# Attention scores and weight transposes of a fused attention and expert kernel, cut in halves of 64 queries

## The chip, the cores and the metric

The kernel runs on one core of one Trainium2 chip. The metric is the device time of one execution in microseconds. TensorE (PE in the profile) does the matmuls; its weight loads are listed as PEld. VectorE is DVE, ScalarE is ACT, GpSimd is POOL, and SP is the queue that issues most of the DMAs. PSUM is the memory that matmuls write.

## What is computed

Three stages follow one another: attention over pooled keys and values, a dense layer with an ELU, and a layer of eight experts of which each token uses one.

```python
B, H, S, D = 8, 8, 576, 64
k_p = k.reshape(B, H, 72, 8, D).mean(axis=3)      # v_p likewise
scores = (1 / 8) * q @ k_p.T                       # 576 x 72 per batch and head
attn = softmax(scores)
x = (attn @ v_p) laid out as 4608 x 512            # tokens x (heads * 64)
h = x @ w_in;  y = elu(h) @ w_out                  # 512 -> 2048 -> 512
e = argmax(y @ w_gate)                             # one of 8 experts
out = gate * relu(y @ w1[e]) @ w2[e]
```

Everything is float32 in and out. The two dense layers multiply in three products of a high and a low part; scores, transposes and the product with the values are plain float32 matmuls.

## The kernel before

**Tiles.** The 4608 tokens are 36 query tiles of 128 tokens. A batch has 576 = 4.5 x 128 tokens, so tiles 4, 13, 22 and 31 hold 64 queries of one batch and 64 of the next; the other 32 belong to one batch. Three query tiles make a block of 384 tokens, and a block has 16 steps, one for each 128 columns of the hidden layer.

**Attention of a tile t.** `s_mm` (L405) multiplies the queries `qT` (stationary, heads in pairs: one head of a pair on partitions 0 to 63, the other on 64 to 127) with the pooled keys `kT` (72 columns move) into two PSUM banks `sp`, one for each half of the partitions. `parts(t)` gives one run of 128 queries, or two runs of 64 for the four tiles that straddle two batches. DVE takes the maxima (L414), ACT the exponentials (L423), DVE normalises (L427 to L429). `t_mm(t, hh)` (L435) transposes the 128 x 72 weights of four heads into one bank `aTp`; it is called for `hh` 0 and 1. `t_copy` (L441) copies each bank to SBUF as `aT`. `pv_mm` (L450) multiplies `aT` with the pooled values into a bank `pv`, and `pv_copy` (L463, L464) splits that into the block's `xh` and `xl`.

**Order.** The order on every engine of this phase is the order in which the code is written. `first_block` does tiles 0 to 2, and the scores of tile 3. Then `step(n)` issues: the 12 matmuls of the first dense layer into `h` (`g1_mm`, L477), the slot `pe_mid`, the activations on ACT (L487 to L489) and DVE (L494, L495), the slot `act_mid`, the 9 matmuls of the second dense layer into `y` for step n - 2 (`g2`, L519), the slot `pe_end`, and so on. A table fills the slots: from tile 9 on, scores stand in `pe_mid` of step s, transposes in `pe_mid` of step s + 3, their two copies in `act_mid` of that step, behind the activations, and `pv_mm` in its `pe_end`. So TensorE has in such a step: `h`, transposes, `y`, `pv`. Tiles 6 to 8 have places of their own (transposes in `pe_end`). During the first 28 steps DVE and ACT also decode the dense weights (`dec`, `raw`, L217 to L242).

**Banks.** `bank` hands out three PSUM banks in turn (and, in the first block, three more) to scores, transposes and `pv`. A tile takes two for scores, two for transposes and one for `pv`.

The last third of the time is the expert stage (lines from 1000 on), which the change does not touch.

Of the kernel before, what the change touches and what calls it, by code (L numbers as in the profile page):

```python
# [19 lines left out]
P = 128  # L20
B, H, S, D = 8, 8, 576, 64
POOLW = 8
SP = S // POOLW
# [27 lines left out]
NT_MAIN = 3  # L51
NU_MAIN = 3
UT = P // 4
SIDES = (5, 6, 8)

C_ID = 0
# [17 lines left out]
def constants():  # L74
# [13 lines left out]
    c[:, C_E:C_E + NE] = e  # L88
    c[:, C_J] = p // UT
    c[p, C_SUM + SUM_AT + p // POOLW] = 1  # L90
# [4 lines left out]
def fused_kernel(ctx: ExitStack, tc: tile.TileContext, q, k, v, w_in, w_out, w_gate, w1, w2, cst, out):  # L95
    nc = tc.nc
# [10 lines left out]
    ident = cpool.tile([P, P], F32, name="ident")  # L107
# [63 lines left out]
    kTs = [apool.tile([P, 4, SP], F32, name=f"kT{i}") for i in range(2)]  # L171
# [104 lines left out]
    def bank(shape, name):  # L276
        early["n"] += 1
        if early["bank"] and early["n"] % 2:
            return bank_y(shape, name)
        return bank_a(shape, name)  # L280
# [90 lines left out]
    banks = {}  # L371

    qTs, ss, aTs = {}, {}, {}
    xh, xl = {}, {}

    def parts(t):
        r0 = t * P
        b0 = r0 // S
        n0 = min(P, (b0 + 1) * S - r0)
        res = [(b0, r0 - b0 * S, 0, n0)]  # L380
        if n0 < P:
            res.append((b0 + 1, 0, n0, P - n0))
        return res
# [9 lines left out]
    def s_mm(t):  # L393
        ss[t] = (
            work([P, H, SP], "s", f"s{t}"),
            ring(apool, [P, H], F32, "mx", 3, f"mx{t}"),
            ring(apool, [P, H], F32, "sm", 3, f"sm{t}"),
        )
        ps = [bank([P, 4, SP], f"sp{t}_{o}") for o in range(2)]
        qT = qTs.pop(t)  # L400
        for pr in range(4):
            for b, s0, p0, n in parts(t):
                for o in range(2):
                    os = slice(D * o, D * (o + 1))
                    nc.tensor.matmul(  # L405
                        ps[o][p0:p0 + n, pr], qT[os, pr, p0:p0 + n], kTs[b % 2][os, pr], start=True, stop=True
                    )
        for o in range(2):
            banks["s", t, o] = ps[o]
        if t < 6:  # L410
            w_free(f"qT{t}")
# [16 lines left out]
        nc.vector.reciprocal(sm, sm)  # L428
        nc.vector.tensor_mul(s, s, sm.unsqueeze(2).to_broadcast([P, H, SP]))  # L429

    def t_mm(t, hh):
        s = ss[t][0]
        ps = banks["t", t, hh] = bank([P, 4, P], f"aTp{t}_{hh}")
        for h in range(4):
            nc.tensor.transpose(ps[:SP, h], s[:, 4 * hh + h], ident)  # L435

    def t_copy(t, hh, copy):
        ps = banks.pop(("t", t, hh))
        if hh == 0:
            aTs[t] = work([SP, H, P], "aT", f"aT{t}")  # L440
        copy(aTs[t][:, 4 * hh:4 * hh + 4], ps[:SP])  # L441

    def pv_mm(t):
        aT = aTs.pop(t)
# [220 lines left out]
    def at(n, slot, fn, *args):  # L665
        events.setdefault((n, slot), []).append((fn, args))
# [11 lines left out]
        at(n, "dve_mid" if t in SCORE0 else "end", s_norm, t)  # L678

    def trans_at(t, n):  # L680
        for hh in range(2):
            at(n, "pe_end" if t in OUT else "pe_mid", t_mm, t, hh)
            at(n, "act_end" if t in OUT else "act_mid", t_copy, t, hh, nc.scalar.copy)
        out = OUT.get(t, ((n, "pe_end"), (n + 1, "pre")))
        at(*out[0], pv_mm, t)
        at(*out[1], pv_copy, t)
# [4 lines left out]
    OUT = {  # L691
        6: ((28, "pe_end"), (29, "pre")),
        7: ((29, "pe_end"), (30, "pre")),
        8: ((31, "pe_mid"), (31, "act_mid")),
    }
# [23 lines left out]
    for n, t in enumerate(range(TB, 2 * TB)):  # L719
        if n:  # L720
            at(n, "pe_mid", s_mm, t)
            for hh in range(2):
                at(n, "dve_late", s_max, t, hh)
        for hh in range(2):
            at(n, "act_mid" if n else "pre", s_exp, t, hh)
        at(n, "act_end" if n else "dve_pre", s_norm, t)
        for hh in range(2):
            at(n + 1, "pe_mid", t_mm, t, hh)
            at(n + 1, "act_hi", t_copy, t, hh, (nc.scalar.copy, nc.vector.tensor_copy)[hh])
        at(n + 1, "pe_end", pv_mm, t)  # L730
        at(n + 1, "copies", pv_copy, t)
# [15 lines left out]
    for x, (w, c) in enumerate(chunks):  # L747
        n = 2 + x
# [76 lines left out]
    def first_block():  # L825
# [23 lines left out]
            for hh in range(2):  # L849
                s_max(t, hh)  # L850

        def trans(t):
            for hh in range(2):
                t_mm(t, hh)

        for pr in range(4):
            prep_k(0, pr)
        k_scale(0)
# [16 lines left out]
        exps(2)  # L875
        a_load(5)
        s_norm(0)
        trans(0)
        v_sum(0, range(2, 4))
        w_hi(0, 0)  # L880
        t_copy(0, 0, nc.scalar.copy)
        t_copy(0, 1, nc.scalar.copy)
        w_mul(0, 1, nc.vector.tensor_scalar_mul)
        s_norm(1)
        trans(1)
        v_sum(0, range(4, 5))
        v_sum_copy(0)
        s_norm(2)
        pv_mm(0)
        trans(2)  # L890
        t_copy(1, 0, nc.scalar.copy)
        t_copy(1, 1, nc.scalar.copy)
        w_bits(0, 1)
# [98 lines left out]
    def lists_rest():  # L992
# [5 lines left out]
        nb = new([P, NE], "nb")  # L998
        nc.vector.tensor_scalar(nb, rest, float(UT), None, op0=ALU.is_gt)
        nt = new([P, NE], "nt")  # L1000
# [53 lines left out]
    def m_index(it):  # L1054
# [5 lines left out]
        if kind == "U":  # L1060
            for j in range(4):
                nc.sync.dma_start(oi[UT * j:UT * (j + 1), 0:1], tab[bass.ds(b0, UT), :])
        else:
# [182 lines left out]
    def u_g1(it):  # L1246
# [3 lines left out]
        for c in range(KC):  # L1250
            for j in range(4):
                js = slice(UT * j, UT * (j + 1))
                mark["g1"] = nc.tensor.matmul(
                    ps[js], z[:, c, :UT], raws2[it, j][0][:, c], start=c == 0, stop=c == KC - 1
                ).ins
# [109 lines left out]
    for k in range(1, len(main)):  # L1365
        kind, prev = main[k][0], main[k - 1][0]
        for u in range(TILES[kind]):
            if kind == "T":
                n = 4 * k - 2
            elif prev == "T":  # L1370
                n = 4 * k - TILES[kind] + u
            else:
                n = 4 * k - 1
# [170 lines left out]
```

## Time and profile before

| | us |
|---|---|
| median of 3 runs | 1417.66 |
| lowest, highest run | 1416.53, 1419.87 |
| the profiled execution | 1418.04 |
| its span, first to last instruction | 1416.2 |
| mean granted TensorE clock | 0.995 |

The profiled execution took 1.8 us more than its span, and 0.4 us more than the median. In a timeline row the columns are start, duration, engine, line, operation, names, shapes and count; rows that follow each other with the same names are merged. A matmul's duration includes its modelled way through the array, so matmuls overlap, and what a group costs is read from the start of one group to the start of the next. In brackets stands idle time before the instruction and what ended it.

### The profile page before, as it was taken

The numbers are of one execution on the slowest core, as the hardware profiler recorded it, in microseconds if no ns is written. First come the engines' busy times: TensorE is split into PE (matmuls) and PEld (weight loads), VectorE is DVE, ScalarE is ACT, GpSimd is POOL, SyncE is SP. The second block draws the span as 40 slices with busy tenths as digits, with TensorE's granted clock in tenths as the row PEclk, the third lists the DMA queues.
The fourth block names the chain that finished last, engine by engine and source line by source line (L and its number), as shares of the span: only waits on it lengthen the run. The fifth ranks groups of instructions, "written<-read, shape, count | busy, mean of one in ns | idle before, by whom it ended". The sixth has DMA issues, their size and how long they took to land. (4 is left out here: it accounts for less than half of the span.)

```text
span 1416.2 us, 22675 instructions
## 1 busy us (share of the span) xinstructions
PE 1396.7 (99%) x8113; PEld 1197.3 (85%) x8114; DVE 913.4 (64%) x2152; ACT 741.7 (52%) x1781; POOL 199.1 (14%) x207
## 2 busy tenths in 40 slices
PE   9999999999999999999999999999999999999996
PEld 6798888888888888888888888988888888778785
DVE  6899877876766667576757576886556444434261
ACT  5777755655656556566565565562333333334251
POOL 0011010111111211121210000020222122112020
PEclk9999999999999999999999999999999999999999
DMA  9156435566452552543451332364566456759460
GB/s 344 57 174 198 134 72 97 66 75 99 59 89 47 92 59 49 76 75 67 85 73 53 53 46 46 88 163 105 172 94 205 127 162 240 239 185 330 144 222 23
DMA packets 109141, 169.37 MB, mean 120 GB/s; under 512 B 15510, under 2 KB 53016, under 8 KB 109017
## 3 DMA queue, kind: packets, MB, share of 16 engines
q1 hardware_dynamic: 91528, 135.45, 38.2%
q0 software_dynamic: 17488, 32.37, 11.1%
q8 instruction: 66, 1.08, 0.4%
q14 instruction: 59, 0.48, 0.2%
HBM read 146.35 MB, written 21.88 MB: 119 GB/s over the span
## 5 line engine op out<-in xcount | busy, mean ns | idle before, releaser
L519 PE MATMUL y<-woh,gh 128*128 128x512 f32 x576 | 232.5, 404 | 1.9 <-DVE yr L533 1.9
L519 PE MATMUL y<-woh,gl 128*128 128x512 f32 x576 | 227.5, 395 | 0.0
L519 PE MATMUL y<-wol,gh 128*128 128x512 f32 x576 | 226.1, 392 | 0.0
L494 DVE SCALAR_TENSOR_TENSOR g<-g,th 128x384 f32<-128x384 f32 x192 | 106.6, 555 | 160.7 <-ACT th L489 159.7
L570 DVE SCALAR_TENSOR_TENSOR junk<-yr,wgb 128x512 bf16<-128x512 f32 x264 | 181.2, 686 | 3.5 <-ACT yr L535 1.3
L487 ACT ACTIVATE th<-h 128x384 f32<-128x384 f32 x192 | 94.5, 492 | 165.7 <-PE h L477 165.4
L477 PE MATMUL h<-xh,wih 128*128 128x384 f32 x768 | 170.0, 343 | 1.4 <-ACT xh L463 1.4
L477 PE MATMUL h<-xl,wih 128*128 128x384 f32 x768 | 165.4, 337 | 0.0
L477 PE MATMUL h<-xh,wil 128*128 128x384 f32 x768 | 164.8, 336 | 0.0
L501 ACT CAST gh<-g 128x384 fp32r<-128x384 f32 x192 | 98.9, 515 | 115.7 <-DVE g L495 96.2
L477 PEld LDWEIGHTS h<-xh,wih 128*128 128x128 f32 x768 | 136.8, 189 | 19.5 <-issue 2.7
L1187 DVE SCALAR_TENSOR_TENSOR hlD<-mhD,hhD 128x512 fp32r<-128x512 f32 x64 | 44.2, 690 | 161.4 <-ACT hhD L1186 153.9
L1186 ACT ACTIVATE hhD<-mhD 128x512 fp32r<-128x512 f32 x64 | 38.5, 601 | 199.3 <-PE myD L1209 191.6
L477 PEld LDWEIGHTS h<-xl,wih 128*128 128x128 f32 x768 | 136.6, 188 | 0.2
L477 PEld LDWEIGHTS h<-xh,wil 128*128 128x128 f32 x768 | 136.6, 188 | 0.0
L502 DVE TENSOR_TENSOR gl<-g,gh 128x384 fp32r<-128x384 f32 x192 | 107.1, 558 | 39.9 <-ACT gh L501 36.1
L519 PEld LDWEIGHTS y<-woh,gl 128*128 128x128 f32 x576 | 108.4, 188 | 23.8
L519 PEld LDWEIGHTS y<-woh,gh 128*128 128x128 f32 x576 | 108.3, 188 | 21.1 <-issue 2.4
L519 PEld LDWEIGHTS y<-wol,gh 128*128 128x128 f32 x576 | 108.7, 189 | 16.9
L495 DVE TENSOR_TENSOR g<-g,h 128x384 f32<-128x384 f32 x192 | 106.3, 554 | 6.6
L489 ACT ACTIVATE th<-th 128x384 f32<-128x384 f32 x192 | 100.8, 525 | 6.1
L488 ACT ACTIVATE g<-th 128x384 f32<-128x384 f32 x192 | 100.8, 525 | 6.1
(275 smaller groups left out, 2313.6 us busy)
## 6 DMA issues: line engine op xcount, KB each, us to landing
wgb<-in_moe_w_gate_dram SPq DMA_DIRECT2D x96, 256.0 KB, 4.8
w1stD<-in_moe_w_dram SPq DMA_DIRECT2D x32, 512.0 KB, 3.6
w2stD<-in_moe_w_dram SPq DMA_DIRECT2D x32, 512.0 KB, 7.8
qT<-in_q_dram SPq DMA_DIRECT2D x36, 256.0 KB, 9.6
ybuf<-yr SPq DMA_DIRECT2D x33, 256.5 KB, 7.1
raw<-in_moe_w_in_dram SPq DMA_DIRECT2D x16, 512.0 KB, 7.8
raw<-in_moe_w_out_dram SPq DMA_DIRECT2D x15, 512.0 KB, 8.6
t1U<-in_moe_w_dram SPq DMA_DIRECT2D x12, 512.0 KB, 7.7
```

The lines of the kernel that those rows point to most:

```text
L477: mark["g1"] = nc.tensor.matmul(ps, wi[i][a][:, c, o:o + P], bb[blk][:, c, :], start=n == 0, stop=n == 3 * KC - 1).ins
L487: nc.scalar.activation(th, hps[blk, f], AF.Relu, scale=-1.0)
L488: nc.scalar.activation(g, th, AF.Exp, scale=-1.0)
L489: nc.scalar.activation(th, th, AF.Tanh, scale=-0.5)
L494: nc.vector.scalar_tensor_tensor(g, g, 1.0, th, op0=ALU.add, op1=ALU.mult)
L495: nc.vector.tensor_max(g, g, hps.pop((blk, f)))
L501: nc.scalar.copy(gh, g)
L502: nc.vector.tensor_sub(gl, g, gh)
L519: nc.tensor.matmul(ys[blk][j], a[:, js], wo[i][bb][:, o, :], start=n == 0 and f in FIRST[blk], stop=n == 2 and f in LAST[blk],)
L570: nc.vector.scalar_tensor_tensor(junk, yrows[blk][j][:, :DM], 1.0, pes[blk, e], op0=ALU.mult, op1=ALU.mult, accum_out=lgs[blk][:, j, e:e + 1])
L1186: nc.scalar.activation(hh, ps, AF.Relu)
L1187: nc.vector.scalar_tensor_tensor(hl, ps, 0.0, hh, op0=ALU.max, op1=ALU.subtract)
```

## The change

The scores of all tiles are computed in halves of 64 queries, as those of the four straddling tiles were. A half's stationary operand is 64 x 64 and writes 64 PSUM partitions, so two heads and two halves are four quarters of the array. The transposes of a tile are issued as one group of 16 in place of two groups of 4: each transposes 64 queries of one head, from partitions 0 to 63 or 64 to 127, with the matching 64 x 64 corner of the identity as moving operand. The two halves of the queries go into two banks, `aTp..._0` and `aTp..._1`, each with all eight heads. A copy now takes one half of the queries of all heads in place of all queries of four heads.

```diff
+HQ = P // 2
...
         for pr in range(4):
-            for b, s0, p0, n in parts(t):
+            for q in range(2):
+                b = (P * t + HQ * q) // S
+                qs = slice(HQ * q, HQ * (q + 1))
                 for o in range(2):
                     os = slice(D * o, D * (o + 1))
-                    nc.tensor.matmul(
-                        ps[o][p0:p0 + n, pr], qT[os, pr, p0:p0 + n], kTs[b % 2][os, pr], start=True, stop=True
-                    )
+                    nc.tensor.matmul(ps[o][qs, pr], qT[os, pr, qs], kTs[b % 2][os, pr], start=True, stop=True)
...
-    def t_mm(t, hh):
+    def t_mm(t):
         s = ss[t][0]
-        ps = banks["t", t, hh] = bank([P, 4, P], f"aTp{t}_{hh}")
-        for h in range(4):
-            nc.tensor.transpose(ps[:SP, h], s[:, 4 * hh + h], ident)
-
-    def t_copy(t, hh, copy):
-        ps = banks.pop(("t", t, hh))
-        if hh == 0:
+        pss = [bank([P, H, HQ], f"aTp{t}_{q}") for q in range(2)]
+        for h in range(H):
+            for q in range(2):
+                qs = slice(HQ * q, HQ * (q + 1))
+                nc.tensor.transpose(pss[q][:SP, h], s[qs, h], ident[qs, qs])
+        for q in range(2):
+            banks["t", t, q] = pss[q]
+
+    def t_copy(t, q, copy):
+        ps = banks.pop(("t", t, q))
+        if q == 0:
             aTs[t] = work([SP, H, P], "aT", f"aT{t}")
-        copy(aTs[t][:, 4 * hh:4 * hh + 4], ps[:SP])
+        copy(aTs[t][:, :, HQ * q:HQ * (q + 1)], ps[:SP])
...
     def trans_at(t, n):
+        at(n, "pe_end" if t in OUT else "pe_mid", t_mm, t)
         for hh in range(2):
-            at(n, "pe_end" if t in OUT else "pe_mid", t_mm, t, hh)
             at(n, "act_end" if t in OUT else "act_mid", t_copy, t, hh, nc.scalar.copy)
```

The scores of tile 12 on TensorE, behind the last matmuls of the dense layer's `h`, before (the number behind `sp`, `aTp` and `aT` is the tile):

```order
L477 MATMUL h3_0_3008<-xh3_2373,wil0_213 128x384 x4
L405 MATMUL sp12_0_3024<-kT0_98,qT12_2753 128x72
L405 MATMUL sp12_1_3025<-kT0_98,qT12_2753 128x72
L405 MATMUL sp12_0_3024<-kT0_98,qT12_2753 128x72
L405 MATMUL sp12_1_3025<-kT0_98,qT12_2753 128x72
```

And at the same place now:

```order
L482 MATMUL h3_0_3192<-xh3_2525,wil0_221 128x384 x4
L408 MATMUL sp12_0_3208<-kT0_98,qT12_2929 64x72
L408 MATMUL sp12_1_3209<-kT0_98,qT12_2929 64x72
L408 MATMUL sp12_0_3208<-kT0_98,qT12_2929 64x72
L408 MATMUL sp12_1_3209<-kT0_98,qT12_2929 64x72
```

The place is the same; two pairs of heads took the four rows before, and one pair takes them now, so a tile has 16 rows in place of 8.

The transposes of tile 12 on TensorE, three steps later, before, with the first matmuls of `y` behind them:

```order
L477 MATMUL h3_3_3162<-xh3_2373,wil1_396 128x384 x4
L435 MATMUL aTp12_0_3175<-ident_68,s12_3021 72x128 x4
L435 MATMUL aTp12_1_3180<-ident_68,s12_3021 72x128 x4
L519 MATMUL y3_0_3138<-woh0_448,gh3_1_3107 128x512
L519 MATMUL y3_0_3138<-wol0_449,gh3_1_3107 128x512
```

And now, the first five of 16, before the same two rows of `y`:

```order
L482 MATMUL h3_3_3354<-xh3_2525,wil1_452 128x384 x4
L438 MATMUL aTp12_0_3367<-ident_68,s12_3205 72x64
L438 MATMUL aTp12_1_3368<-ident_68,s12_3205 72x64
L438 MATMUL aTp12_0_3367<-ident_68,s12_3205 72x64
L438 MATMUL aTp12_1_3368<-ident_68,s12_3205 72x64
L438 MATMUL aTp12_0_3367<-ident_68,s12_3205 72x64
```

The two banks are now written in turn, so the first bank is complete one instruction before the last and no longer halfway through.

The copies of tile 12 on ACT, behind the activations of their step, before:

```order
L487 ACTIVATE th3_3_3186<-h3_3_3162 128x384
L488 ACTIVATE g3_3_3185<-th3_3_3186 128x384
L489 ACTIVATE th3_3_3186<-th3_3_3186 128x384
L441 COPY aT12_3192<-aTp12_0_3175 72x512
L441 COPY aT12_3192<-aTp12_1_3180 72x512
```

And now:

```order
L492 ACTIVATE th3_3_3386<-h3_3_3354 128x384
L493 ACTIVATE g3_3_3385<-th3_3_3386 128x384
L494 ACTIVATE th3_3_3386<-th3_3_3386 128x384
L446 COPY aT12_3392<-aTp12_0_3367 72x8x64
L446 COPY aT12_3392<-aTp12_1_3368 72x8x64
```

Nothing moved on ACT; a copy writes eight runs of 64 elements in place of one run of 512. POOL and SP are unchanged too, and so is DVE, but for weights of three expert tiles, T5 to T7, each of which changes places with the instruction behind it on ACT and DVE; the `myT` matmuls of the profile (24 of each kind, 8 for a tile) show that three such tiles run, T0 to T2.

## Rows read from the trace of the kernel before

**Rows 1.** The page, busy time by engine.
```profile
PE 1396.7 (99%) x8113; PEld 1197.3 (85%) x8114; DVE 913.4 (64%) x2152; ACT 741.7 (52%) x1781; POOL 199.1 (14%) x207
```
**Rows 2.** Waits of PE, 60 to 1416 us: total us, times, longest us.
```profile
PE y L519 <- DVE yr L533: 1.9, 1, 1.9
PE sp L405 <- ACT aT L441: 1.1, 1, 1.1
...
PE pv L450 <- ACT aT L441: 0.3, 1, 0.3
```
**Rows 3.** Timeline of PE: the two longest of these waits.
```profile
140.92 0.47 PE L519 MATMUL y<-woh,gh 128*128 128x512 f32 x1 [1.93 <-DVE yr L533]
...
151.81 1.11 PE L405 MATMUL sp<-kT,qT 64*128 64x72 f32 x14 [1.07 <-ACT aT L441]
```
**Rows 4.** Busy time in the stretch of the steady blocks, 157 to 880 us.
```profile
157.00:880.00 723.00, 722.70 (x4437) 640.09 (x4436) 508.29 (x1324) 432.21 (x1172) 89.49 (x97) 1.00 0.44 70
```
**Rows 5.** Groups of PE instructions by form, with busy us and mean ns.
```profile
L435 PE MATMUL aTp<-ident,s 128*72 128x128 f32 x288 | 37.3, 272 | 0.3 <-issue 0.3
...
L1104 PE MATMUL zTD<-ident,xgD 128*128 128x128 f32 x128 | 17.2, 272 | 0.0
```
**Rows 6.** Timeline of PE at the scores of a tile of one batch.
```profile
318.75 0.86 PE L477 MATMUL h<-xh,wil 128*128 128x384 f32 x4
...
320.92 0.39 PE L519 MATMUL y<-wol,gh 128*128 128x512 f32 x1
```
**Rows 7.** Timeline of PE at the scores of a straddling tile.
```profile
294.93 0.85 PE L477 MATMUL h<-xh,wil 128*128 128x384 f32 x4
...
295.71 0.73 PE L405 MATMUL sp<-kT,qT 64*64 64x72 f32 x32
...
296.37 0.50 PE L519 MATMUL y<-woh,gh 128*128 128x512 f32 x1
...
296.71 0.40 PE L519 MATMUL y<-wol,gh 128*128 128x512 f32 x1
```
**Rows 8.** Timeline of PE at the transposes of a tile.
```profile
308.29 0.86 PE L477 MATMUL h<-xh,wil 128*128 128x384 f32 x4
308.98 1.03 PE L435 MATMUL aTp<-ident,s 128*72 128x128 f32 x8
309.77 0.48 PE L519 MATMUL y<-woh,gh 128*128 128x512 f32 x1
310.09 0.40 PE L519 MATMUL y<-wol,gh 128*128 128x512 f32 x1
```
**Rows 9.** Timeline of PE at `pv` of a straddling tile.
```profile
312.03 1.15 PE L450 MATMUL pv<-aT,v 72*64 72x64 f32 x32
313.11 0.96 PE L477 MATMUL h<-xh,wih 128*128 128x384 f32 x4
```
**Rows 10.** Timeline of ACT and PEld in the same step, from activations to `pv`.
```profile
309.24 0.49 ACT L487 ACTIVATE th<-h 128x384 f32<-128x384 f32 x1 [0.78 <-PE h L477]
...
310.75 1.05 ACT L441 COPY aT<-aTp 72x512 f32<-72x512 f32 x2
...
312.02 1.01 PEld L450 LDWEIGHTS pv<-aT,v 72*64 72x64 f32 x32 [0.36 <-ACT aT L441]
```
**Rows 11.** Groups of ACT: the two copies out of PSUM, with mean ns.
```profile
L441 ACT COPY aT<-aTp 72x512 f32<-72x512 f32 x68 | 35.9, 576 | 0.0
...
L463 ACT CAST xh<-pv 128x512 fp32r<-128x512 f32 x36 | 21.2, 588 | 14.3 <-PE pv L450 14.1
```
**Rows 12.** Timeline in the first block: DVE after scores, PE at transposes.
```profile
11.63 0.82 DVE L414 TENSOR_REDUCE mx<-sp 128x4 f32<-128x288 f32 x2 [1.29 <-PE sp L405]
...
22.51 1.07 PE L435 MATMUL aTp<-ident,s 128*72 128x128 f32 x8
23.51 1.09 PE L450 MATMUL pv<-aT,v 72*64 72x128 f32 x16
```
**Rows 13.** Busy time in one stretch; behind POOL's the granted clock (PEclk).
```profile
150.00:160.00 10.00, 8.93 (x46) 7.46 (x45) 8.03 (x18) 8.65 (x29) 0.83 (x1) 0.83 0.62 174
```

More of the change, by code (lines that the diff above doesn't have):

```diff
@@ L726, in fused_kernel @@
         at(n, "act_end" if n else "dve_pre", s_norm, t)
+        at(n + 1, "pe_mid", t_mm, t)
         for hh in range(2):
-            at(n + 1, "pe_mid", t_mm, t, hh)
             at(n + 1, "act_hi", t_copy, t, hh, (nc.scalar.copy, nc.vector.tensor_copy)[hh])
@@ L850, in maxs @@
                 s_max(t, hh)
-        def trans(t):
-            for hh in range(2):
-                t_mm(t, hh)
         for pr in range(4):
@@ L877, in first_block @@
         s_norm(0)
-        trans(0)
+        t_mm(0)
         v_sum(0, range(2, 4))
@@ L884, in first_block @@
         s_norm(1)
-        trans(1)
+        t_mm(1)
         v_sum(0, range(4, 5))
@@ L889, in first_block @@
         pv_mm(0)
-        trans(2)
+        t_mm(2)
         t_copy(1, 0, nc.scalar.copy)
```

## The prediction, made before the changed kernel was run

> **What bounds the kernel now.** I read the page's busy times first: TensorE is busy 1396.7 of 1416.2 us, VectorE 64% and ScalarE 52% of the span [rows 1]. A busy TensorE may still be a slow one, so the list of its waits came next. From 60 us to the end the waits that matter here are one of 1.9, one of 1.1 and one of 0.3 us [rows 2], and in the 723 us of the steady blocks it was busy for 722.7, with VectorE at 508 and ScalarE at 432 [rows 4]. So from about 157 us on time is the sum of what TensorE's groups take from start to start, and a group that gets shorter shortens the kernel, as long as no wait takes its place. The first 157 us are mixed: there the change's groups stand in chains with the other engines, and two of the waits lie there, the one for `yr` that ends at 140.9 us, and that of tile 7's scores for the copies `aT` of tile 6, over at 151.8 [rows 3].
>
> **Scores.** The new form is in the trace already, in the four straddling tiles. From the start of the last four `h` matmuls to the second `y` matmul behind the scores, a tile of one batch takes 320.92 - 318.75 = 2.17 us [rows 6], a straddling tile 296.71 - 294.93 = 1.78 us [rows 7], both between the same neighbours. The stretch holds the way into the small tiles and out again, so nothing is hidden in the difference of 0.39 us: 32 matmuls of 64 x 64 are faster than 16 of 64 x 128. (Each float32 product is two instructions.) The straddling tiles' instructions are those that every tile has now, in the same order; only `kT` is one buffer in place of two. Of the 32 tiles that change, 0 to 3 belong to the first block, 5 to the first steps, and 6 stands before the wait for `yr`. Tile 7, most of whose scores follow the second wait, and the tiles from 8 to 35 without 13, 22 and 31 are 26: 26 x 0.39 = 10.1 us.
>
> The rows show 32 instructions of such scores in 0.66 us, 0.021 us each [rows 7]. The Trainium skill speaks against cutting matmuls this small: in TensorE: Matmul & The Clock Gate, section "Wait — 56ns, not 53.3ns?", it says that a matmul decoded in microcode costs its sequencer about 62 ns, however small it is. By that, 32 would take at least 1.98 us (an estimate from the page), and the change would lose over a microsecond per tile; the trace disagrees, and the sum goes by the rows.
>
> Tile 6 gives nothing, I think: the wait that follows it ends with VectorE's additions for `yr`, which come last in a queue of weight decoding. Tile 6's transposes are taken up likewise by the wait for their own copies [rows 3].
>
> **Transposes.** The trace has no transpose from 64 partitions. Today a tile takes 310.09 - 308.29 = 1.80 us from the last four `h` to the second `y` [rows 8]: 0.69 to the first transpose, 0.79 for eight, 0.32 to the second `y`. Around small tiles the two ends are longer: 295.71 - 294.93 = 0.78 on the way in, and 296.71 - 296.37 = 0.34 behind [rows 7]. Between them I need the price of eight pairs, each a pair of row halves. Two blocks of the trace have such halves in turn, on rows or on columns: the straddling scores, eight rounds of four with 72 moving columns in 0.66 us [rows 7], and the straddling `pv`, 16 rounds of two with 64 moving columns in 1.08 us [rows 9]. If a round costs the same in both, it is (1.08 - 0.66) / 8 = 0.053 us, and 0.24 us are filling and draining. What sets the round? A transpose with 128 columns of weights costs as much as one with 72 (17.2 / 128 = 0.134 and 37.3 / 288 = 0.130 us busy, both 272 ns long [rows 5]), so the moving columns do, and these are 64. Eight rounds are then 0.24 + 8 x 0.053 x 64 / 72 = 0.61 us. The whole is 0.78 + 0.61 + 0.34 = 1.73 us, only 0.07 less than now: transposes over all 128 rows have `h` and `y` as neighbours in the same form and pay neither the way in nor the way out, and the halves pay both. Bounds: if the weights' columns set the round, 72 for 64, the block is 0.24 + 0.42 x 72 / 64 = 0.71 and the tile 0.03 slower; half of today's 0.79 would be the most that two halves at once can give, 0.28 less. I take the 0.07.
>
> That is 29 tiles (7 to 35) less the one whose `pv` the wait list shows held by the copies [rows 2]: 28 x 0.07 = 2.0 us.
>
> **The copies.** They now start with both banks complete at the end of the group, not the first halfway. That costs nothing in a steady step, because ScalarE does three activations first: these start 0.95 us behind the start of the last `h` matmuls, the copies at 310.75, about 1 us behind the last transpose, and end at 311.80. The load of `pv` follows at 312.02 [rows 10]. It could move forward by these 0.22 us less a semaphore's way, which is more than 0.07, and limits what the faster bound above could give to some 0.2 a tile. A copy now writes runs of 64 elements. The cast to `xh`, which writes four separate runs, takes 588 ns for 128 partitions, the copy 576 [rows 11], so I expect no difference, and an increase of 0.07 each would be the point from which `pv` waits.
>
> **The first block.** Here VectorE waited 1.29 us for the scores of tile 1 [rows 12], and the chain runs over the maxima, the normalisation and the transposes of tile 0. Scores 0 and 1 shorten it by 0.39 each. The transposes of tile 2 take 1.00 us between two `pv` groups [rows 12], where both ways in and out are paid already, so the halves save 1.00 - 0.61 = 0.39; scores of tile 3 stand between `pv` groups too, 0.39. Together 1.6 us. In the steps behind, `pv` of tile 3 and the scores of tile 5 wait for copies, and give little. I take 1.5; the bounds are 0, if loads or decoding set the pace, and 1.5.
>
> **The clock.** The stretch from 150 to 160 us shows a granted clock of 0.83 [rows 13]: a third of it ran at 1.2 GHz in place of 2.4, some 1.7 us lost. It follows the two waits above, and both become a little longer. I leave the clock as it is, with 1.7 us either way as bounds (that stretch gone, or one more).
>
> **The sum.** 10.1 + 2.0 + 1.5 = 13.6 us. Against the profiled execution of 1418.04 us (span 1416.2 and 1.8 around it) this makes 1404.4 us; that execution lies 0.4 above the median, which is within the runs shown. A measurement of this kernel can tell about 0.2%, 2.8 us, from no change.
>
> **Rivals.**
> 1. Halves of transposes don't run side by side. Then 16 follow each other at half of today's price each, 0.79 in all behind the filling of 0.24: 0.78 + 1.03 + 0.34 = 2.15 us, 0.35 more than now, 28 x 0.35 = 9.8 lost. With 10.1 and 1.5 gained: 1416.2 us. For it: no transpose of the trace is in halves. Against: scores and `pv` alternate halves without this.
> 2. A transpose's price is not its columns, and a half costs as much as a whole one now, 0.79 / 8 = 0.099 us [rows 8], none beside another. Then the group is 16 x 0.099 + 0.24 = 1.82 us, the tile 2.94, 1.14 more than now, 28 x 1.14 = 32: with 10.1 and 1.5 gained 1438 us. It decides from 0.41 us per tile on, where 28 tiles take back 11.6 us: that is a group of 1.09 us, or 0.053 for each half on average. This is the case that is slower than before. For it: no row has such a half. Against: both forms of scores and `pv` run at 0.02 to 0.03 us an instruction [rows 7, 9]. The Trainium skill's price of a small matmul, in the section named above, is a rule of this kind: 16 x 0.062 + 0.24 = 1.23 us would be an estimate by it.
> 3. Half of the scores' gain returns as waits, of `pv` for slower copies or of scores for their bank: 5 us less, 1409.4. For it: the copies end only 0.22 us before `pv` loads. Against: ScalarE is busy 432 of 723 us and waited 0.78 us for `h` in that very step [rows 4, 10].
> 4. The scores gain nothing, since TensorE was not the bound: 1418. Against it are the 722.7 of 723 us [rows 4].
>
> **Chances.** The forecast 0.77, rival 1 0.07, rival 2 0.05, rival 3 0.09, rival 4 0.02. Only rivals 1 and 4 are within 0.2%, rival 2 is slower: faster 0.86, same 0.09, slower 0.05. The likeliest time is 1404.4. Its own range: downward 1.7 for the clock and 28 x 0.13 for transposes that reach the copies' limit of 0.2, 1399; upward 1.5 for the first block, 2.8 for transposes at 0.71 and 1.7 for the clock, 1410.4. Both extremes at once are unlikely; 1400.5 to 1410 holds this case almost whole and rival 3, and that is some 8 in 10.
>
> **What would show it.** In the steady blocks the scores of every tile should read as in the straddling ones: 1.78 us from the last `h` to the second `y`, 32 instructions in 0.66. The transposes should read x16 in about 0.6 us, with 0.78 before and 0.34 behind, 1.73 in all. The copies should take 576 ns still and end more than 0.1 us before `pv`; TensorE's wait list from 157 us on should stay below 1 us. The first `h` should start some 1.5 us earlier. The prediction is wrong if the transposes' group takes over 0.8 us, if the copies grow, or if the waits for `yr` and of tile 7's scores grow by more than the time won before them.

## The result: 0.8% faster, and the profile of the changed kernel

The changed kernel takes 1406.48 us (median of 4 runs, 1405.62 to 1408.48), the kernel before 1417.53 beside it: a ratio of 0.9918, with a 95% interval of 0.9904 to 0.9931. In a second set of runs it was 0.9912 (0.9898 to 0.9926), the median 1405.91 of 5 runs against 1418.62. The gain is 11 to 12.7 us where 13.6 were forecast, and the time lies inside the range. The profiled execution took 1406.9 us, with a span of 1405.1. The page's row for the engines, to be held against [rows 1]:

```profile
PE 1382.5 (98%) x8913; PEld 1173.6 (84%) x8914; DVE 915.2 (65%) x2152; ACT 742.0 (53%) x1781; POOL 197.0 (14%) x207
```

TensorE has 800 more matmuls and is busy for 14.2 us less; VectorE and ScalarE are within 2 us of before. In the steady blocks it is still the bound. The windows of the changed kernel for the same steps as in [rows 4], in the same columns:

```profile
157.00:867.00 710.00, 708.57 (x5053) 617.88 (x5053) 509.53 (x1325) 431.28 (x1167) 88.60 (x97) 1.00 0.43 71
```

TensorE is idle for 1.4 of 710 us here, where it was idle for 0.3 of 723. The list of its waits from 60 us on (total us, times, longest) names these 1.4:

```profile
PE y L524 <- DVE yr L538: 2.3, 1, 2.3
PE pv L455 <- ACT aT L446: 1.4, 3, 0.8
PE myT L1210 <- DVE gateS L1102: 0.7, 1, 0.7
PE myT L1210 <- DVE hlT L1188: 0.4, 1, 0.4
PE myT L1210 <- ACT hhT L1187: 0.2, 1, 0.2
```

Against [rows 2] the wait of tile 7's scores is gone, that for `yr` is 0.4 longer, and the waits of `pv` for its copies have grown from 0.3 to 1.4 us, in three tiles. The three waits of `myT` are new.

The timeline of TensorE in the changed kernel, at the transposes of a tile and then at the scores of one; the counterparts are [rows 6 to 8]:

```profile
303.08 0.85 PE L482 MATMUL h<-xh,wil 128*128 128x384 f32 x4
303.87 0.64 PE L438 MATMUL aTp<-ident,s 64*72 64x64 f32 x16
304.44 0.50 PE L524 MATMUL y<-woh,gh 128*128 128x512 f32 x1
304.78 0.39 PE L524 MATMUL y<-wol,gh 128*128 128x512 f32 x1
...
313.44 0.86 PE L482 MATMUL h<-xh,wil 128*128 128x384 f32 x4
314.23 0.73 PE L408 MATMUL sp<-kT,qT 64*64 64x72 f32 x32
314.89 0.50 PE L524 MATMUL y<-woh,gh 128*128 128x512 f32 x1
315.22 0.39 PE L524 MATMUL y<-wol,gh 128*128 128x512 f32 x1
```

Both are read from the start of the last four `h` to the second `y`. Scores: 315.22 - 313.44 = 1.78 us, 32 instructions in 0.66, exactly the stretch that the straddling tiles had before. Transposes: 304.78 - 303.08 = 1.70 us, 0.79 to the first transpose, 16 in 0.57, 0.34 to the second `y`. The forecast was 1.73, from 0.78, 0.61 and 0.34; a whole tile took 1.80.

**Where the time went.** Two instructions serve as marks in every trace: the first `h` matmul behind `pv` of tile 7, and that of the last step of the projections. The timeline of TensorE has them here for the kernel before, and below for the changed one:

```profile
181.88 0.62 PE L477 MATMUL h<-xh,wih 128*128 128x384 f32 x2
...
946.61 0.87 PE L477 MATMUL h<-xh,wih 128*128 128x384 f32 x4
```
```profile
178.13 0.61 PE L482 MATMUL h<-xh,wih 128*128 128x384 f32 x2
...
933.39 0.69 PE L482 MATMUL h<-xh,wih 128*128 128x384 f32 x3
```

Up to the first mark the changed kernel wins 3.75 us, between the marks 764.73 - 755.26 = 9.47, so it is 13.2 us ahead at the last step, where the prediction's sum would have it 13.6 ahead. Behind that it gives 2.1 us back in this execution: the spans differ by 11.1. In between stand the three waits of `myT` above, in the expert stage. Whether they belong to the program is a question for the experiments.

The 764.73 and 755.26 us can be cut by kind, from the start of each matmul to the start of the next, and added up (27 groups of scores and 28 of transposes stand between the marks; the kinds that have no row sum to 80.2 to 80.6 us in all four; the last two columns are experiments that follow, each with one half of the change):

| us between the marks | before | changed | scores only | transposes only |
|---|---|---|---|---|
| scores with the ways in and out | 34.2 | 25.1 | 25.1 | 34.3 |
| transposes with the ways in and out | 27.1 | 23.5 | 27.0 | 23.6 |
| from `y` to `pv` | 9.3 | 10.3 | 9.1 | 10.5 |
| among `h` | 311.7 | 313.1 | 313.8 | 311.6 |
| among `y` | 301.9 | 303.0 | 302.0 | 302.6 |
| all | 764.7 | 755.3 | 757.1 | 763.0 |

The scores give 9.1 us and the transposes 3.6. Against that stand 1.1 us that `pv` waits, 1.4 us by which `h` takes longer and 1.1 by which `y` does; some 0.6 of the last is the second `y` behind the transposes, which starts 0.34 us behind the first and not 0.32 as in [rows 8].

### The profile page after: what moved, and what is told of

It reads as the page before. It is cut to its first block, busy times and chain, and to the rows that moved or that the text cites. A ratio compares the mean times of both kernels' runs of the same rounds, so it can differ in the third digit from the quotient of the medians.

```text
span 1405.1 us, 24287 instructions
## 1 busy us (share of the span) xinstructions
PE 1382.5 (98%) x8913; PEld 1173.6 (84%) x8914; DVE 915.2 (65%) x2152; ACT 742.0 (53%) x1781; POOL 197.0 (14%) x207
```

## The experiments

In the table each kernel stands against the kernel before on its own chip. The last column is the time between the two marks in its profile. It is the steadiest measure: the granted clock is 1.00 all the way from 175 to 950 us in each of these traces, and the waits of the expert stage lie behind the second mark.

| kernel | median us | runs | ratio to before, 95% | between the marks |
|---|---|---|---|---|
| before | 1417.5 to 1419.9 | 4 to 23 | 1 | 764.7 |
| changed | 1406.48 | 4 | 0.9918 (0.9904 to 0.9931) | 755.3 |
| changed, again | 1405.91 | 5 | 0.9912 (0.9898 to 0.9926) | 756.1 |
| scores only | 1406.88 | 5 | 0.9923 (0.9911 to 0.9936) | 757.1 |
| transposes only | 1415.62 | 11 | 0.9983 (0.9975 to 0.9992) | 763.0 |
| first tiles only | 1415.25 | 11 | 0.9979 (0.9970 to 0.9988) | 764.6 |
| joined | 1400.54 | 6 | 0.9888 (0.9872 to 0.9904) | 751.6 |
| joined, whole transposes | 1400.95 | 4 | 0.9876 (0.9861 to 0.9891) | 749.4 |
| extra half | 1441.98 | 5 | 1.0168 (1.0153 to 1.0183) | 786.7 |
| extra whole | 1425.52 | 5 | 1.0046 (1.0032 to 1.0060) | 770.4 |
| copies early | 1404.65 | 5 | 0.9900 (0.9881 to 0.9918) | 753.7 |
| behind `pv`, mended | 1404.05 | 5 | 0.9893 (0.9877 to 0.9908) | 754.1 |

**Scores only** (against the changed kernel; the copies are by heads again as well):

```diff
-        for h in range(H):
-            for q in range(2):
-                qs = slice(HQ * q, HQ * (q + 1))
-                nc.tensor.transpose(pss[q][:SP, h], s[qs, h], ident[qs, qs])
+            for hh in range(2):
+                ps = banks["t", t, hh] = bank([P, 4, P], f"aTp{t}_{hh}")
+                for h in range(4):
+                    nc.tensor.transpose(ps[:SP, h], s[:, 4 * hh + h], ident)
```

> Scores in halves in every tile as in the changed kernel, transposes whole with copies by heads as before. Nothing is left out. My sum: the scores carry 10.1 us and the first block about 1.1, so 1417.5 - 11.2 = 1406.3; but the changed kernel's trace gives the transposes about 2 us of its 11.05, so by that reading this kernel takes 1408.5 (1407.8 to 1409.5). Rival: the waits of pv for the later copies and the longer h matmuls eat all that the halves of the transposes save, and it takes 1406.5 like the changed kernel, or less.

Measured: 1406.88, 10.9 us below the kernel before. Between the marks it wins 7.6 of the changed kernel's 9.5. By the time alone the rival would stand: the transposes in halves add nothing that the two intervals can tell. By the marks they add 1.9 us, in that pair of traces, of which `h` (table above) makes up 0.7; against the second trace of the changed kernel it is 1.0 us, of which `h` makes up 0.9.

**Transposes only**, the other half of the diff on the kernel before (`parts(t)` sets the runs of the scores again):

```diff
-            for q in range(2):
-                b = (P * t + HQ * q) // S
-                qs = slice(HQ * q, HQ * (q + 1))
+            for b, s0, p0, n in parts(t):
```

> Transposes in halves as in the changed kernel, scores as before. Nothing is left out. Theory: 28 tiles by 0.07 to 0.10 us and 0.4 in the first block, less some waits of pv for copies: 1417.5 - 2.4 = 1415.1 (1414.3 to 1416.0); the group x16 at about 0.57 us with longer ways in and out on both sides of it. Rival 1: halves and ways cancel, 1417.5. Rival 2: the copies, which now start together, hold pv in many tiles, and it is slower than 1417.5.

Measured: 1415.62, 2.2 us below before, and 1.8 between the marks. (Its profiled execution took 1417.5, more than the median, and reaches the first mark 0.9 us later than before, so the gain of 0.4 that was expected of the first block does not show in this trace.) The table by kind has the reason why it is not more between the marks: the groups themselves give 3.5, `pv` takes back 1.2 and `y` 0.7. The interval excludes both rivals as they stand, but the mechanism of rival 2, `pv` held by its copies, is there with 1.2 us. With the scores alone in halves it is not there (9.1 us from `y` to `pv`, before 9.3), so the transposes and their copies bring it.

**First tiles only** (`t < 6` chooses the new form, in scores, transposes and copies):

> Both edits for tiles 0 to 5 alone, the rest as before. Nothing is left out. Theory: the first h starts 1.5 to 2.5 us earlier, VectorE's chain of additions keeps about 1.3 of it up to the wait for yr, and the rest of the kernel is unchanged: 1417.5 - 1.3 = 1416.2, or 1414.5 if the wait of tile 7's scores and the half-clock stretch behind it vanish as in the changed kernel. Rival: the time won is taken up whole by the wait for yr, 1417.5.

Measured: 1415.25, 2.6 us below before; the marks are as far apart as before, as they must be. Up to the step of the long wait for `yr` this trace is 1.2 us ahead, and behind it 2.5. The windows of 130 to 160 us show what happened there (they are read as [rows 13]):

```profile
130.00:150.00 20.00, 18.02 (x94) 15.76 (x92) 17.07 (x33) 13.55 (x38) 3.33 (x4) 1.00 0.50 132
150.00:160.00 10.00, 9.37 (x56) 8.52 (x57) 8.05 (x18) 7.89 (x28) 0.83 (x1) 1.00 0.56 145
```

The granted clock is 1.00 where it was 0.83 before [rows 13]: the stretch at 1.2 GHz behind the two waits is gone in this execution. In the changed kernel's trace it has moved, to beside the wait for `yr`, and the one in the first block is longer (a granted clock of 0.72 from 28 to 40 us, where before had 0.86):

```profile
28.00:40.00 12.00, 11.01 (x105) 10.39 (x107) 9.75 (x20) 7.84 (x20) 1.14 (x2) 0.72 0.99 352
136.00:144.00 8.00, 5.73 (x22) 4.69 (x21) 7.65 (x15) 4.66 (x15) 1.67 (x2) 0.79 0.51 128
```

**Changed, again.** No edit.

> The changed kernel once more, unaltered. In its first trace it was 13.2 us ahead of the kernel before at the last step of the projections and only 11.0 us at its end, with three waits of TensorE in the expert stage that the kernel before does not have. Theory A: this loss belongs to the program, and the trace shows it again; 1406.5 (1405.5 to 1408.5). Theory B: it belongs to that one execution; this trace keeps the 13 us to the end, and the time is about 1404.5.

Measured: theory B for the loss. This trace is 12.4 us ahead at the last step and 12.1 in the span. Its list of waits from 60 us on:

```profile
PE pv L455 <- ACT aT L446: 2.2, 3, 0.9
PE y L524 <- DVE yr L538: 2.0, 1, 2.0
```

No `myT` waits, so those belong to that execution, and of the 2.1 us only 0.3 come again. The median, though, is not 1404.5 but 1405.91. What recurs, and grows, is the wait of `pv` for the copies: 2.2 us in three tiles. It is the most that any wait takes in the steady blocks, and the prediction had set it to nothing.

**Copies early.** The next run goes after these waits. The timeline of ScalarE in the changed kernel shows one of them building up, in a step in which a block is routed:

```profile
328.23 0.22 ACT L603 ACTIVATE lg<-lg 128x24 f32<-128x24 f32 x1 [2.99 <-DVE lg L602]
328.35 0.50 ACT L506 CAST gh<-g 128x384 fp32r<-128x384 f32 x1
328.76 0.48 ACT L492 ACTIVATE th<-h 128x384 f32<-128x384 f32 x1
329.27 0.53 ACT L493 ACTIVATE g<-th 128x384 f32<-128x384 f32 x1
329.83 0.53 ACT L494 ACTIVATE th<-th 128x384 f32<-128x384 f32 x1
330.26 1.05 ACT L446 COPY aT<-aTp 72x512 f32<-72x512 f32 x2
```

ScalarE waits 2.99 us for VectorE's `lg`, a value of the router, with `gh` of the step before, three activations and the two copies queued behind it. So the copies begin at 330.26, 2.0 us behind the last transposes, whose banks were full long ago, and `pv` starts at 331.36 in place of 330.56. In the step that the prediction read, ScalarE waits for `h` and not for VectorE [rows 10].

That ScalarE is late is not new, though: in the same step of the kernel before it waits 3.03 us for `lg`. What is new is which copy `pv` needs. The copies and the start of `pv` in that step, before and then changed:

```profile
335.92 1.05 ACT L441 COPY aT<-aTp 72x512 f32<-72x512 f32 x2
336.54 1.14 PE L450 MATMUL pv<-aT,v 72*64 72x128 f32 x16 [0.29 <-ACT aT L441]
```
```profile
331.36 0.44 PE L455 MATMUL pv<-aT,v 72*64 72x128 f32 x4 [0.80 <-ACT aT L446]
```

Before, `pv` starts 0.62 us behind the start of the two copies, when the first is done: that copy held four heads with all their queries, enough for the first matmuls of `pv`. Now it starts 1.10 us behind (331.36 - 330.26), when both are done, since a copy holds half the queries of every head and a matmul of `pv` reads all 128 queries of a head. The other traces agree: in six of seven with whole transposes the earliest `pv` starts 0.62 to 0.68 us behind the start of its copies (in the seventh, extra half, 1.11), and in the seven with halves none starts under 1.10. So each late step costs up to 0.48 us more; an estimate from these starts is that in the two traces of the changed kernel 1.2 and 1.4 us of what `pv` waits in the three steps would be gone if its copies were still cut by heads. No run has halves with copies cut by heads.

The edit puts the copies behind `gh` and ahead of the activations:

```diff
-            at(n, "act_end" if t in OUT else "act_mid", t_copy, t, hh, nc.scalar.copy)
+            at(n, "act_end" if t in OUT else "dve_pre", t_copy, t, hh, nc.scalar.copy)
```

> The changed kernel with the copies aT of the tiles from 9 on ahead of the three activations of their step on ScalarE, behind the cast gh of the step before, in place of behind them. Nothing is left out. Theory: the three waits of pv (1.4 and 2.2 us in the two traces of the changed kernel) come from ScalarE reaching the copies late in steps in which VectorE is late; with the copies 1.6 us earlier they go, and the time is 1406.2 - 1.8 = 1404.4 (1403.5 to 1405.5). Rival 1: VectorE sets the pace in these steps anyway, and the wait turns up at the next y or h instead, 1406.2. Rival 2: the activations that now come 1.05 us later hold up y in more steps, and it is slower than 1407.

Measured: 1404.65, and between the marks 753.7, 1.5 and 2.4 us less than in the two traces of the changed kernel, which is what `pv` waited in them (1.4 and 2.2). The same place in this kernel's timeline of ScalarE, and its whole list of TensorE's waits from 157 to 870 us:

```profile
326.13 0.22 ACT L603 ACTIVATE lg<-lg 128x24 f32<-128x24 f32 x1 [3.00 <-DVE lg L602]
326.26 0.50 ACT L506 CAST gh<-g 128x384 fp32r<-128x384 f32 x1
326.67 1.06 ACT L446 COPY aT<-aTp 72x512 f32<-72x512 f32 x2
327.62 0.49 ACT L492 ACTIVATE th<-h 128x384 f32<-128x384 f32 x1
```
```profile
PE pos L639 <- DVE acc L628: 0.2, 1, 0.2
```

The wait for `lg` is there as before, the waits of `pv` are gone, and only 0.2 us at `pos` came in their place: both rivals fall in the trace. With the copies this early `pv` never waits for the second one, so the run shows that late copies hold `pv`; it does not tell how much of the lateness is ScalarE's and how much is the new cut of the copies. The ratio, 0.9900, lies 0.0012 to 0.0018 below those of the changed kernel, and the intervals overlap; the marks tell it, the time alone does not.

**Extra half and extra whole.** These measure the price of the way in and out by itself, on the kernel before: one transposition of the identity, unused, in each of 54 steps that have nothing between `h` and `y`.

```diff
+    def x_mm(n):
+        ps = bank([P, 4, P], f"x{n}")
+        nc.tensor.transpose(ps[:SP, 0, :64], ident[:64, :SP], ident[:64, :64])
+
+    for t in range(3 * TB, NT):
+        for d in (1, 2):
+            at(SCORE[t][0] + d, "pe_mid", x_mm, SCORE[t][0] + d)
```

> The kernel before, with one more transposition of 64 rows of the identity into a bank of its own in 54 steps of the steady blocks that have no attention work between h and y; its result is not used. Nothing is left out. Theory: a lone half pays a fixed way in and out of the row halves, 0.09 us longer before it and 0.14 us longer behind it by the changed kernel's trace, and about 0.05 us for itself: 54 x 0.28 = 15 us, 1433 (1429 to 1436). Rival: there is no fixed price, and what a group of halves shows at its two ends belongs to its many instructions; then a half costs about half of a whole one, 54 x 0.05 = 2.7 us, 1420.5.

The other has `nc.tensor.transpose(ps[:SP, 0], ident[:, :SP], ident)`.

> The same with a whole transposition of 128 rows in each of the 54 places. Nothing is left out. Theory: 54 x 0.10 = 5.4 us, 1423.2 (1421 to 1425), since a whole one has h and y as neighbours in its own form. Rival: any fp32 transposition between h and y costs a fixed price of its own, and this is as slow as the half, 1433.

Measured: 23.4 and 6.9 us more than before, 22.0 and 5.7 between the marks. The timeline of TensorE at one such place, first with a half, then with a whole one, and last such a step of the kernel before:

```profile
303.26 0.87 PE L477 MATMUL h<-xh,wil 128*128 128x384 f32 x4
304.06 0.24 PE L715 MATMUL x<-ident 64*72 64x64 f32 x1
304.24 0.50 PE L519 MATMUL y<-woh,gh 128*128 128x512 f32 x1
304.58 0.39 PE L519 MATMUL y<-wol,gh 128*128 128x512 f32 x1
```
```profile
302.18 0.85 PE L477 MATMUL h<-xh,wil 128*128 128x384 f32 x4
302.88 0.27 PE L715 MATMUL x<-ident 128*72 128x128 f32 x1
302.90 0.48 PE L519 MATMUL y<-woh,gh 128*128 128x512 f32 x1
303.22 0.40 PE L519 MATMUL y<-wol,gh 128*128 128x512 f32 x1
```
```profile
299.95 0.85 PE L477 MATMUL h<-xh,wil 128*128 128x384 f32 x4
...
300.88 0.40 PE L519 MATMUL y<-wol,gh 128*128 128x512 f32 x1
```

From the last four `h` to the second `y` it is 1.32 us with a half and 1.04 with a whole one; without either, a step takes 0.93. So a whole transposition costs 0.11 us and a half 0.39: the smaller instruction is 3.5 times as dear. The instruction alone is not the reason, since 16 halves in one group take 0.57 us, 0.036 each; what is left is that its two neighbours have another form. The rivals of both runs fall. The half's time lies far above its theory's range, too. The 0.28 was too low by what a whole one costs, 0.11: it put together differences to whole transposes, which are not free themselves. The Trainium skill names a mechanism in TensorEngine Tiling (Array Packing), section "Key Properties": changing the tiling mode drains TensorE. The traces agree in that the two changes around a lone half cost 0.28 us more than a whole one, which needs none; that a drain is what takes this time, no run here shows.

**Joined.** If the price is one of the visit, two groups in one visit share it. Scores of the tiles from 10 on move directly behind `pv` of the tile before, which is in small tiles too:

```diff
-            SCORE[t] = (NF * (blk - 1) + 5 * j, "pe_mid")
-            TRANS[t] = SCORE[t][0] + 3
+            n0 = NF * (blk - 1) + 5 * j
+            SCORE[t] = (n0 - (2 if j else 3), "pe_end") if t > 9 else (n0, "pe_mid")
+            TRANS[t] = n0 + 3
```

> The changed kernel, with the scores of the tiles from 10 on moved up to stand directly behind the pv of the tile before (and, for the first tile of a block, behind the last pv of the block before), so that two groups of small tiles share one way in and one way out. Nothing is left out. Theory: the ways in and out cost about 0.2 us per tile by themselves, and 26 tiles save 5 us: 1406.5 - 5 = 1401.5 (1400.5 to 1403.5). Rival 1: the price of a group lies in its own instructions and moving it changes nothing, 1406.5. Rival 2: the scores wait for their banks or hold up the copies of pv, and the kernel is slower than 1406.5.

Measured: 1400.54, by the medians faster than both kernels. Two of its six runs, 1404.85 and 1406.18, come up to the times of the changed kernel, and the intervals of the ratios touch or overlap; between the marks it is 3.7 and 4.5 us shorter than the two traces of that kernel. The timeline of TensorE:

```profile
380.05 1.09 PE L455 MATMUL pv<-aT,v 72*64 72x128 f32 x16
381.07 0.73 PE L408 MATMUL sp<-kT,qT 64*64 64x72 f32 x32
381.73 0.79 PE L482 MATMUL h<-xh,wih 128*128 128x384 f32 x3
```

The two together take 1.68 us to the next `h`. Apart they take 1.02 and 1.78 - 0.93 = 0.85, so 0.19 is saved, 26 times: 5 us, of which the marks show 3.7 against the first trace of the changed kernel. Part of the rest is one idle stretch of 1.3 us before a `y` for which the profile names no releaser.

**Joined, whole transposes**: the same edit on the kernel with scores only.

> The joined kernel (scores in halves, from tile 10 on directly behind the pv of the tile before), with the transposes whole as before and copied by heads. Nothing is left out. Theory: the halves of the transposes are worth the 2 us in the steady steps that scores alone lost against the changed kernel, so 1400.5 + 2 = 1402.5 (1401.5 to 1403.5). Rival: their gain is taken back by pv waiting for copies, and this takes 1400.5 or less.

Measured: the rival's time, within 0.5 us. 1400.95 against 1400.54 on another chip, as ratios 0.9876 against 0.9888 with intervals that overlap, and between the marks it is 2.2 us shorter. No `pv` waits in it, but that is a small part: cut by kind, the transposes in halves give 3.7 us in the joined kernel, and against them stand 0.7 from `y` to `pv`, the idle stretch of 1.3, and 1.7 among `h` and 1.9 among `y` that no wait explains (0.7 of the latter is the second `y` behind the halves). So which of the two is better is not shown; once the scores are joined, no run here shows a gain from the halves of the transposes.

**Behind `pv`.** Two runs had the transposes of the tiles from 14 on directly behind `pv` of the tile before, where the halves pay no way in of their own; the second had them whole:

```diff
+            if t > 13:
+                SCORE[t] = (n0 - (5 if j else 6), "pe_mid")
+                TRANS[t] = SCORE[t][0] + 3
+            else:
+                SCORE[t] = (n0 - (t - 9), "pe_mid")
+                TRANS[t] = SCORE[t][0] + 3
+            if t > 9:
+                OUT[t] = ((n0 + 3, "pe_end"), (n0 + 4, "pre"))
```

> The changed kernel with scores and transposes of the tiles from 14 on one tile earlier, so that the transposes in halves stand directly behind the pv of the tile before, and pv of a tile comes five steps behind its own transposes (tiles 10 to 13 lead up to this by 1 to 4 steps). Nothing is left out. Theory: the halves no longer pay a way in between h and y (0.12 per tile by the rows, 22 tiles, 2.6 us), and no pv waits for its copies any more (1.5 to 2.2 us): 1406.2 - 4.5 = 1401.7 (1400.5 to 1403). Rival 1: the place does not matter and only the waits of pv go, 1404.4. Rival 2: scores wait for banks that pv and transposes hold, 1406 or more.

> The same places, with the transposes whole as before and copied by heads; scores in halves. Nothing is left out. Theory: here a whole transpose has nothing to save, since it paid no way between h and y either, and it still takes 0.34 us longer in its own instructions, of which the halves give back 0.12 on the way out to h: 22 x 0.22 to 22 x 0.34, so 4.8 to 7.5 us slower than the same places with halves, about 1407. Rival: the halves are worth no more here than between h and y (0.13 per tile, 3 us): 1404.5.

Both expectations err on one point: with this edit the loads of batch 3's keys begin one step before tile 8 reads those of batch 1 in the same buffer, so the scores of tile 8 are others, and with them its routing and the work of the expert stage. Their times, 1453.52 and 1457.61 us, are not comparable. The steps between the marks do not depend on values: 754.2 with halves, 758.2 whole. The 4.0 us are 0.18 for each of the 22 tiles, below the theory's 0.22 to 0.34 and near the rival's 0.13. Cut by kind, the transposes with their ways are 6.2 us shorter with halves, an estimated 0.25 for each of the 22 tiles, which the theory has right; 1.3 of it comes back mostly as waits around `pos` and 1.0 among `h` and from `y` to `pv`. With the loads two steps later for that batch:

```diff
-            at(n0 - 22 + j, "end", k_link, b, j)
+            at(n0 - (20 if b == 3 else 22) + j, "end", k_link, b, j)
```

> Transposes in halves directly behind the pv of the tile before, as in the run with that name before, but with the loads of batch 3's keys two steps later, behind the scores of tile 8 that still read batch 1's in their place. Nothing is left out. Theory, from the steady steps of that run, which the keys' values do not touch: it starts the last step of the projections 1.0 us earlier than the changed kernel's first trace and has its expert stage, 1405.4 (1404 to 1407). Rival: the loss of 2.7 us in the steps 38 to 62 came from the lead-up and goes with the later loads, 1402.7.

Measured: 1404.05, a ratio of 0.9893 (0.9877 to 0.9908), between the marks 754.1 as in the run ahead of it. By the marks the theory holds and the rival's mechanism falls: the later loads change nothing. The time alone does not decide: 1404.05 is at the low end of the theory's 1404 to 1407, and the ratio, on the 1417.53 us of the first set, would be 1402.4, beside the rival's 1402.7. TensorE waits 1.7 us here for banks that VectorE has yet to empty (`pos` behind `xl`). Between the marks the place is worth 1.2 us against the first trace of the changed kernel, less than joined scores with 3.7.

## Why the prediction was right, and where it was off

**TensorE is the bound, time is the sum of its groups.** Right. The kernel became faster by what its groups became shorter, less what came back as waits, and every experiment between the marks adds up in the same way, but for `h` and `y` of another length without a wait (below). That 13.2 us at the last step came so near to 13.6 is in part luck: up to the first mark the sum had some 2.4 us (the first block, and tiles 7 and 8) where 3.75 were won, and between the marks 11.3 where 9.5 were.

**The scores, 26 x 0.39 = 10.1.** Right in mechanism and size: 1.78 us in all tiles, 9.1 for the 27 groups between the marks, of which three had the form already, so 0.38 for each of 24; with the scores alone 10.9 us were measured, the first block included. Reading the price from four tiles of the old trace that had the new form, between the same neighbours, is what made this term exact. By the Trainium skill's 62 ns per microcoded matmul (TensorE: Matmul & The Clock Gate, section "Wait — 56ns, not 53.3ns?") a tile's scores would take it to 0.78 + 1.98 + 0.34 = 3.10 us, 0.93 more than now and not over a microsecond, and 16 half transposes would take at least 0.99 us, both estimates from that page; the trace shows 1.78 and 0.57. The page gives that price for hardware decode switched off, so the trace does not contradict it: it shows that the price is not one of these matmuls.

**The transposes, 28 x 0.07 = 2.0.** The group was nearly right, 0.57 us for 0.61, by two errors that cancel: by the starts in the trace a pair of halves takes 0.056 us, where 0.053 x 64 / 72 = 0.047 were forecast, and what comes on top is 0.12 and not 0.24. The ways in and out were right: 0.10 saved per tile, 2.8 us for the 28 between the marks. The extra half shows that the ways, which eat most of the gain, come with the visit, however little is in it. Only "pay neither the way in nor the way out" was too strong for whole transposes: one alone costs 0.11 us, most of it in a later second `y`.

**The copies.** This is the step that failed: "That costs nothing in a steady step, because ScalarE does three activations first". It was read in one step, in which ScalarE waits for `h`, and it looked at when the copies can start, not at which of them `pv` needs. In three steps with router work on VectorE, ScalarE waits for VectorE and copies late, before as now; but before, the first copy was enough for `pv` to start, 0.62 us behind the start of the copies, and now it takes both, 1.10 us. So the waits grew from 0.3 to 1.4 and 2.2 us, and the forecast's own sign, a wait list below 1 us from 157 us on, failed. The copies did not grow (578 ns for 576). Copies early shows that late copies are what holds `pv`; the share of the new cut is read from the starts and not from a run of its own. Of the 2.8 us some 1 to 1.8 are left, and in the time (changed against scores only) less than the intervals can tell. The likeliest case held with the mechanism of rival 3 in it: gain that returns as waits of `pv` for copies, 1.1 to 1.9 us more than before where that rival had 5, and because `pv` needs both of two late copies, not because they take longer.

**The first block, 1.5.** The first `h` came 2.4 us earlier, where 1.5 were forecast, but from the second step on the lead was 0.9 to 1.4 us, and 1.6 just before the wait for `yr`: near the forecast. Behind that wait nothing was left of it for two steps, with 0.4 us more wait and a granted clock of 0.79 from 136 to 144 us; it came back by the place where the kernel before waits for tile 7's scores and runs at 0.83. In the time the first tiles alone are worth 2.6 (1.7 to 4.3 by the interval), and in its trace the lead grows from 1.2 to 2.5 us where before ran at a granted clock of 0.83; the prediction had that as a bound of 1.7, not in the sum.

**Not in the sum at all**: `h` and `y` that take longer without any wait, some 1.4 us for `h` in the first trace, and 0.6 for the second `y` behind transposes in halves.

**Rivals.** 1 and 2 are excluded by 16 halves in 0.57 us, 4 by the result. Something like rival 2 is real for a lone half, 0.39 us against 0.11, though as a price of the visit: what saves the change is that sixteen share one.

## What to carry to other kernels

- When an instruction's form changes, price the visit and not the instruction: the last matmul ahead to the second matmul behind. Here a lone half cost 0.28 us more than a whole transposition, and two groups that share a visit saved 0.19, so first put visits together (3.7 us between the marks here), then make what is in them smaller.
- Before a wait is set to nothing because one step shows slack, list that step's queue in each kind of step. The steps in which another engine has extra work are the ones where the slack is gone. And when a copy is cut another way, ask what its reader needs before it can start: here the first copy was enough before, and now it takes both.
- Where the old trace has a few instances of the new form, take the price from there, over a stretch that holds both its ends.

## What was not expected of the hardware

The same 12 matmuls of `h`, where they follow `y`, take one of three lengths, without a wait in sight: 11 intervals between their starts sum to 1.909, 1.921 or 1.944 us. Steps of one length mostly come in runs. With the first tiles only, nothing differs from the kernel before behind tile 5, and still `h` is longer from 64 to 125 us. The groups of `h` by form in that stretch, first in this kernel, then before (count, busy us, mean ns):

```profile
L494 PE MATMUL h<-xl,wih 128*128 128x384 f32 x60 | 13.0, 338 | 0.0
L494 PE MATMUL h<-xh,wil 128*128 128x384 f32 x60 | 13.0, 337 | 0.0
```
```profile
L477 PE MATMUL h<-xh,wil 128*128 128x384 f32 x60 | 12.9, 336 | 0.0
L477 PE MATMUL h<-xl,wih 128*128 128x384 f32 x60 | 12.8, 335 | 0.0
```

The granted clock is 1.00 in both. Between the marks the `h` of two traces differ by 2.2 us in the table above (311.6 and 313.8), the size of what the transposes in halves are worth. What sets the length stays open; no run here was aimed at it.
